# Tying the conversion of doubles and the combination of stored rows to the pieces of the last chunk

## The chip, the cores and the metric

The kernel runs on one core of one Trainium2 chip. The metric is the device time of one execution in microseconds (us); lower is better. Inputs lie in device memory in the layouts of the host function `_layout`, and the output is written back there.

## The reference

Attention of 2 x 8 heads over 576 positions that keeps the 32 largest scores of each row, then a mixture of 8 experts with gates balanced by eight Sinkhorn rounds, then a second feed-forward layer with Mish. All inputs are float32 for the first two parts. The last layer's weights are doubles in the kernel's input (`w64`, read as 64-bit words).

```python
x = attention_top32(q, k, v)                     # (1152, 512)
logits = x @ w_gate                              # (1152, 8)
P = exp(logits - logits.max())
for _ in range(8):
    P /= P.sum(1, keepdims=True) + 1e-09
    P /= P.sum(0, keepdims=True) + 1e-09
    P *= N / E
for e in range(8):
    out += P[:, e:e+1] * (maximum(x @ w1[e], 0) @ w2[e])   # 512 -> 1024 -> 512
h = out @ w_in                                   # 512 -> 2048
return (h * tanh(softplus(h))) @ w_out           # 2048 -> 512
```

## The kernel before

Tokens come in nine tiles of 128 rows. The first mixture runs over three chunks of tiles, (0, 1), (2, 3) and (4 to 8). Each chunk passes through all 8 experts, and each expert in 8 pieces of 128 hidden columns, so a chunk has 64 pieces (`ffn_pass`). A number is split into a high and a low part of a reduced float type, and a product is three matmuls (high x high, high x low, low x high).

A piece of the last chunk, whose tiles have 640 rows together, is this. Two loads bring its weights (`load_piece`, L517); ScalarE makes the high part `wh` (L520), POOL the low part `wl` of the first half and VectorE that of the second (L522). TensorE computes `h` in two groups of 320 columns, 12 matmuls each, into two PSUM buffers (`mm1`, L619). For each group ScalarE writes `hh` = relu(h) (L537) and VectorE `hl` = relu(h) - hh (L538); the PSUM buffer is free after `hl`. Two pieces later the second product (`second`, 15 matmuls at L596) adds to five PSUM banks `y`, one for each tile. After an expert's 8 pieces `combine` (L638, L640) multiplies each `y` by its gate and adds it to `acc` on VectorE.

The gates are known only when attention has ended, so the first two chunks can't do that: `spill` stores their `y` tiles in device memory, 32 rows in all (8 experts x 4 tiles). The generator `gating` (`gate_logits`, `sinkhorn`, `once_gated`) is advanced by one step at each step of the last chunk. Its end, `once_gated`, loads each stored row into `yb` (two buffers, SP's queue, L735) and combines it (L638, L640). Then it converts the doubles of the last layer's weights, 16 pieces in two halves, so 32 conversions (`double_to_float`, L689 on). A conversion loads 512 KB into `cx` (two buffers, SP's queue, L692), squares the top word on ScalarE into `cd` (L698), does six VectorE operations (L699 and L701 to L705: `cb`, `ca`, `cb`, `cc`, `cc`, `cc`) and stores `cc` on SP's queue (L706). L703 is the last reader of `cx`.

The order on TensorE is the program's. The order on every other engine and queue is a planner's: among the instructions that can go, the one with the best priority goes first, by the streams `first` (0: `hh`, `hl`), `evict` (combinations of `y`), `prep` (weights), `attn` (rows), `moe`, `fill` (conversions). `after(a, b)` adds an edge that puts a behind b in the plan, with no wait on the chip when both are on one engine. Each queue runs in its planned order: an instruction that waits holds up those behind it. Before the change the first VectorE operation of a conversion has one such edge, behind the end of the Sinkhorn rounds (`live["sunk"]`).

After the last chunk the pool of the conversions is closed and its memory goes to the last layer's pools `wq`, `hq` and `mp`. The transposes of the sums (`transposed`) for tiles 0 to 3 are issued from three quarters of the last chunk's steps on.

Of the kernel before, what the change touches and what calls it, by code (L numbers as in the profile page):

```python
# [14 lines left out]
ALU = mybir.AluOpType  # L15
# [32 lines left out]
EARLY = [(t, h) for t in (2, 3) for h in range(H)] + [(t, h) for t in (5, 6) for h in range(HG)]  # L48
EARLY_FROM, EARLY_PER_STEP = 5, 2
HOLD, RATE = 8, 0.25  # L50


class Streams:
# [19 lines left out]
def attention_moe_moe2(ctx: ExitStack, tc: tile.TileContext, qT, kT, vm, vt, wg, wst, w64, out):  # L73
    nc = tc.nc
# [5 lines left out]
    def after(inst, earlier):  # L80

        tc.add_manual_dep(
            inst.ins,
            earlier.ins.name,
            mybir.DependencyInfo(mybir.DependencyClass.NoSync, mybir.DependencyReason.DATA),
            reason="order",
        )
# [24 lines left out]
    with st("attn"):  # L112
# [8 lines left out]
        gate = const.tile([P, NT, E], F32, name="gate")  # L121
# [15 lines left out]
    def groups(n):  # L137

        k = -(-n // 512)
        return [(i * (n // k), n // k) for i in range(k)]  # L140
# [5 lines left out]
    qset, live, away = {}, {}, {}  # L146
# [227 lines left out]
    def bank1(name):  # L374
        if ps_b is None:
            return ps_a.tile([P, 512], F32, tag="tr", name=name)
        return ps_b.tile([P, 512], F32, tag="misc", name=name)

    def gate_logits(ci):

        n = P * len(CHUNKS[ci])
        lt = (const if ps_b is None else yb).tile([2 * E, n], F32, tag="lt", name=f"lt{ci}", bufs=1)
        for c0, m in groups(n):
            with st("attn"):
                ps = bank1(f"lt_{ci}_{c0}")
                k = 0
                for c in range(NC):
                    for x in x_tiles(ci):
                        nc.tensor.matmul(
                            ps[:, :m], wgs[:, c, :], x[:, c, c0 : c0 + m], start=(k == 0), stop=(k == 2 * NC - 1)  # L390
                        )
                        k += 1
                nc.scalar.activation(lt[:, c0 : c0 + m], ps[: 2 * E, :m], AF.Copy)
            yield
        with st("attn"):
            lg = bank1(f"lg_{ci}")[:, : len(CHUNKS[ci]) * 2 * E].rearrange("p (j e) -> p j e", e=2 * E)
            for j, t in enumerate(CHUNKS[ci]):
                nc.tensor.transpose(lg[:, j, :], lt[:, j * P : (j + 1) * P], ident[: 2 * E, : 2 * E])
            t0 = CHUNKS[ci][0]
            nc.scalar.activation(lg16[:, t0 : t0 + len(CHUNKS[ci]), :], lg, AF.Copy)  # L400
        yield
# [65 lines left out]
    def sinkhorn():  # L467
        with st("first"):
            nc.vector.tensor_add(gate, lg16[:, :, :E], lg16[:, :, E:])
            m1 = small.tile([P, 1], F32, tag="m1", name="m1")  # L470
            nc.vector.tensor_reduce(m1, gate.rearrange("p t e -> p (t e)"), AX.X, ALU.max)
            mb = const.tile([P, P], F32, name="mb")
            nc.vector.tensor_copy(mb, m1.to_broadcast([P, P]))
        yield
        with st("first"):
            mt = bank1("mt")[:, :P]
            nc.tensor.matmul(mt, mb, ident, start=True, stop=True)
            gm = small.tile([P, 1], F32, tag="gm", name="gm")
            nc.vector.tensor_reduce(gm, mt, AX.X, ALU.max)
            nc.vector.tensor_scalar(gm, gm, -1.0, None, op0=ALU.mult)  # L480
            nc.scalar.activation(gate, gate, AF.Exp, bias=gm)
        for i in range(8):
            with st("first"):
                rs = small.tile([P, NT], F32, tag="rs", name=f"rs_{i}")
                nc.vector.tensor_reduce(rs, gate, AX.X, ALU.add)
                nc.vector.tensor_scalar(rs, rs, EPS, None, op0=ALU.add)
                nc.vector.reciprocal(rs, rs)
                nc.vector.tensor_mul(gate, gate, rs.unsqueeze(2).to_broadcast([P, NT, E]))
            yield
            with st("first"):  # L490
                cs = bank1(f"cs_{i}")[:, : NT * E]
                nc.tensor.matmul(cs, ones, gate.rearrange("p t e -> p (t e)"), start=True, stop=True)
                cr = small.tile([P, E], F32, tag="cr", name=f"cr_{i}")
                nc.vector.tensor_reduce(cr, cs.rearrange("p (t e) -> p e t", e=E), AX.X, ALU.add)
                nc.vector.tensor_scalar(cr, cr, EPS, None, op0=ALU.add)
                nc.vector.reciprocal(cr, cr)
                nc.vector.tensor_scalar(cr, cr, float(NTOK) / E, None, op0=ALU.mult)
                live["sunk"] = nc.vector.tensor_mul(gate, gate, cr.unsqueeze(1).to_broadcast([P, NT, E]))


    acc = {}
# [24 lines left out]
    class Relu:  # L526
# [8 lines left out]
        def first(self, ps, c0, m):  # L535
            h, l = self.hh[:, c0 : c0 + m], self.hl[:, c0 : c0 + m]
            nc.scalar.activation(h, ps, AF.Relu)  # L537
            nc.vector.scalar_tensor_tensor(l, ps, 0.0, h, op0=ALU.max, op1=ALU.subtract)  # L538

        later = ()  # L540

# [93 lines left out]
    def combine(t, e, y):  # L635
        if t not in acc:
            acc[t] = accb.tile([P, DM], F32, tag=f"acc{t}", name=f"acc_{t}")
            nc.vector.tensor_scalar(acc[t], y, gate[:, t, e : e + 1], None, op0=ALU.mult)  # L638
        else:
            nc.vector.scalar_tensor_tensor(acc[t], y, gate[:, t, e : e + 1], acc[t], op0=ALU.mult, op1=ALU.add)  # L640

    def spill(t, e, y):
        ycount[0] += 1
# [9 lines left out]
    def moe_chunk(ci):  # L653
        for e in range(E):
            put = spill if ci in SPILLED else combine
            yield from ffn_pass(
                f"c{ci}e{e}",
                CHUNKS[ci],
                [wst[p] for p in range(e * EP, (e + 1) * EP)],
                *x_tiles(ci),  # L660
                Relu,
                lambda t, y, e=e, put=put: put(t, e, y),
            )
# [7 lines left out]
    begin = pos = CHUNKS[0][-1] * H + H + AHEAD + 2  # L671
# [17 lines left out]
    def double_to_float(dst, src, name):  # L689

        x = cp.tile([P, 512, 2], U32, tag="cx", name=f"cx_{name}")
        nc.sync.dma_start(x, src.bitcast(U32).rearrange("p (n w) -> p n w", w=2))  # L692
        low, top = x[:, :, 0], x[:, :, 1]
        a = cp.tile([P, 512], U32, tag="ca", name=f"ca_{name}")
        p2 = cp.tile([P, 512], U32, tag="cb", name=f"cb_{name}")
        b = cp.tile([P, 512], F32, tag="cc", name=f"cc_{name}")
        sq = cp.tile([P, 512], F32, tag="cd", name=f"cd_{name}")
        nc.scalar.activation(sq, top.bitcast(F32), AF.Square)  # L698
        begin = nc.vector.tensor_scalar(p2, top, 3, 0x3FFFFFFF, op0=ALU.logical_shift_left, op1=ALU.bitwise_and)  # L699
        after(begin, live["sunk"])  # L700
        nc.vector.scalar_tensor_tensor(a, top, 0xC0000000, p2, op0=ALU.bitwise_and, op1=ALU.bitwise_or)  # L701
        nc.vector.tensor_scalar(p2, a, 0xFF800000, None, op0=ALU.bitwise_and)
        nc.vector.scalar_tensor_tensor(b, low, 2.0**-52, p2.bitcast(F32), op0=ALU.mult, op1=ALU.mult)  # L703
        nc.vector.tensor_add(b, a.bitcast(F32), b)
        nc.vector.scalar_tensor_tensor(b, sq, TINY2, b, op0=ALU.is_ge, op1=ALU.mult)  # L705
        nc.sync.dma_start(dst, b)  # L706
# [19 lines left out]
            yield  # L726

    w32 = []

    def once_gated():  # L730

        with st("attn"):
            for t, e, d in spilled:
                y = yb.tile([P, DM], F32, tag="yback", name=f"yb_{t}_{e}")
                nc.sync.dma_start(y, d)  # L735
                combine(t, e, y)
        with st("fill"):
            for p in range(NPIECE2):
                d = dram.tile([P, PW], F32, tag=f"w32_{p}", name=f"w32_{p}")
                for a in range(PW // 512):  # L740
                    double_to_float(d[:, a * 512 : (a + 1) * 512], w64[p, :, a * 512 : (a + 1) * 512], f"{p}_{a}")
                w32.append(d)
        yield

    steps = 2 * EP * E
    first_rows = transposed(0)
    gating = chain(gate_logits(*live.pop("gate")), sinkhorn(), once_gated())
    for i, _ in enumerate(moe_chunk(len(CHUNKS) - 1)):
        next(gating, None)
        if i >= steps * 3 // 4 and i % 4 == 0:  # L750
            next(first_rows, None)
    for _ in first_rows:
# [24 lines left out]
    for ui, unit in enumerate(UNITS2):  # L777
        rows = transposed(ui + 1) if ui + 1 < len(UNITS2) else iter(())
# [67 lines left out]
```

## Time and profile before

| | |
|---|---|
| median of 3 runs | 1249.01 us (1248.32 to 1250.55) |
| profiled execution | 1249.09 us |
| its span, first to last instruction | 1247.3 us |
| mean granted TensorE clock | 0.993 |
| busy, share of the span | PE 1180.1 us (95%), DVE 858.7 (69%), ACT 648.1 (52%), POOL 546.8 (44%) |
| last chunk's first `h` | 563.3 us |
| last layer's first `h` | 1033.5 us |

PE is TensorE's matmul unit, PEld its weight loads, DVE VectorE, ACT ScalarE, SPq the queue from which the loads are issued. `L619` is line 619 of the kernel; `h_c2e` is tile `h` of chunk 2 (the last), `x24` a count. Matmuls are pipelined and their ends are modelled, so their busy times overlap; where a piece's time matters, it is taken from start to start. Records of neighbouring VectorE operations overlap by up to 0.1 us too.

### The profile page before, as it was taken

To read this page: it belongs to the slowest core of one execution; us is meant where nothing else is said; L and a number is where in the kernel's file an instruction comes from. 1 tells how busy PE (TensorE), PEld (TensorE's weight loads), DVE (VectorE), ACT (ScalarE), POOL (GpSimd) and SP (SyncE) were. 2 spreads that over 40 slices of the span, in tenths; PEclk is the share of its full clock that TensorE was granted. 3 is DMA by queue.
4 is the path that set the end of the run, shared out by engine and by line. 5 is a ranking of instruction groups with operands and counts; after the bars stand their busy time and mean duration, and the time that the engine had idled before them with its cause. 6 is when DMAs were issued, how large, how long until landed. Compare 5 with 4: busy or idle time off the path is not lost.

```text
span 1247.3 us, 20676 instructions
## 1 busy us (share of the span) xinstructions
PE 1180.1 (95%) x7267; PEld 1040.7 (83%) x7267; DVE 858.7 (69%) x1857; ACT 648.1 (52%) x1289; POOL 546.8 (44%) x424
## 2 busy tenths in 40 slices
PE   3678999999999999999999988999999999999998
PEld 2566888998889888889888777899999998889997
DVE  6999999999999999534899989952333332323221
ACT  6786777877777777653233333332323333444432
POOL 7844778877877777771112211121111212222110
PEclk9899999999999999999999999999999999999999
DMA  8444555575655555673278776632222231223201
GB/s 254 121 144 148 178 168 173 178 223 170 213 178 167 163 155 160 186 219 120 79 249 267 237 217 205 217 100 76 77 76 73 72 110 54 91 93 119 76 27 43
DMA packets 105113, 183.18 MB, mean 147 GB/s; under 512 B 14128, under 2 KB 24624, under 8 KB 105008
## 3 DMA queue, kind: packets, MB, share of 16 engines
q1 hardware_dynamic: 103712, 180.68, 46.6%
q8 instruction: 57, 0.93, 0.3%
q10 hardware_dynamic: 1296, 1.18, 0.3%
q14 instruction: 48, 0.39, 0.1%
HBM read 158.55 MB, written 23.27 MB: 146 GB/s over the span
## 4 chain that ended last, share of the span: by engine, by line
PE 66%; DVE 24%; DMA 6%; issue 2%; POOL 1%; ACT 1%; SPq 0%; POOLq 0%; ACTq 0%; DVEq 0%
PE h_c2e L619 12%; PE y_c2e L596 11%; PE h_d L619 8%; PE y_d L596 8%; PE y_c0e L596 7%; PE h_c0e L619 7%; DVE top L254 6%; DVE w L261 5%; PE h_c1e L619 4%; PE y_c1e L596 3%; DMA cx<-in_w_dram 3%; DVE em L290 2%; DVE acc L640 2%; PE pv L348 2%; PE tr L325 1%
## 5 line engine op out<-in xcount | busy, mean ns | idle before, releaser
L522 POOL TENSOR_TENSOR wl_c2e<-wraw_c2e,wh_c2e 128x512 fp32r<-128x512 f32 x64 | 90.7, 1417 | 358.8 <-ACT wh_c2e L520 332.0
L522 POOL TENSOR_TENSOR wl_c1e<-wraw_c1e,wh_c1e 128x512 fp32r<-128x512 f32 x128 | 172.5, 1372 | 52.4 <-ACT wh_c1e L520 49.3
L522 POOL TENSOR_TENSOR wl_c0e<-wraw_c0e,wh_c0e 128x512 fp32r<-128x512 f32 x128 | 171.6, 1356 | 53.0 <-ACT wh_c0e L520 49.9
L619 PE MATMUL h_c2e<-xh,wh_c2e 128*128 128x320 f32 x512 | 161.3, 315 | 14.4 <-DVE hl_c2e L538 14.2
L520 ACT ACTIVATE wh_c2e<-wraw_c2e 128x512 fp32r<-128x512 f32 x128 | 80.7, 630 | 174.5 <-PE y_c2e L596 110.3
L619 PE MATMUL h_c2e<-xl,wh_c2e 128*128 128x320 f32 x512 | 158.7, 310 | 0.0
L619 PE MATMUL h_c2e<-xh,wl_c2e 128*128 128x320 f32 x512 | 158.5, 310 | 0.0
L254 DVE MAX8 top<-w 128x8 f32<-128x576 f32 x216 | 157.7, 747 | 0.8
L596 PE MATMUL y_c2e<-wh_c2e,hh_c2e 128*128 128x512 f32 x320 | 126.6, 396 | 0.5 <-DVE acc L640 0.5
L596 PE MATMUL y_c2e<-wl_c2e,hh_c2e 128*128 128x512 f32 x320 | 125.7, 393 | 0.0
L596 PE MATMUL y_c2e<-wh_c2e,hl_c2e 128*128 128x512 f32 x320 | 125.2, 391 | 0.0
L538 DVE SCALAR_TENSOR_TENSOR hl_c2e<-h_c2e,hh_c2e 128x320 fp32r<-128x320 f32 x128 | 62.1, 485 | 87.2 <-ACT hh_c2e L537 87.0
L619 PEld LDWEIGHTS h_c2e<-xh,wh_c2e 128*128 128x128 f32 x512 | 96.6, 189 | 24.0 <-DVE hl_c2e L538 21.9
L522 POOL TENSOR_TENSOR wl_d<-wraw_d,wh_d 128x512 fp32r<-128x512 f32 x32 | 41.4, 1293 | 161.0 <-ACT wh_d L520 161.0
L520 ACT ACTIVATE wh_c0e<-wraw_c0e 128x512 fp32r<-128x512 f32 x128 | 80.4, 629 | 51.9 <-PE y_c0e L596 21.0
L261 DVE MATCH_REPLACE8 w<-top,w 128x576 f32<-128x576 f32 x144 | 106.3, 740 | 0.0
L619 PEld LDWEIGHTS h_c2e<-xl,wh_c2e 128*128 128x128 f32 x512 | 96.6, 189 | 1.8
L557 DVE TENSOR_TENSOR hl_d<-mg_d,hh_d 128x320 fp32r<-128x320 f32 (+1 forms) x48 | 31.5, 657 | 95.7 <-ACT hh_d L556 95.7
L619 PEld LDWEIGHTS h_c2e<-xh,wl_c2e 128*128 128x128 f32 x512 | 96.7, 189 | 0.0
L520 ACT ACTIVATE wh_c1e<-wraw_c1e 128x512 fp32r<-128x512 f32 x128 | 79.8, 627 | 27.7 <-PE y_c1e L596 11.3
L522 DVE TENSOR_TENSOR wl_c2e<-wraw_c2e,wh_c2e 128x512 fp32r<-128x512 f32 x64 | 47.7, 745 | 66.0 <-ACT wh_c2e L520 65.9
L520 ACT ACTIVATE wh_d<-wraw_d 128x512 fp32r<-128x512 f32 x64 | 40.4, 631 | 95.8 <-PE y_d L596 40.9
(170 smaller groups left out, 3325.5 us busy)
## 6 DMA issues: line engine op xcount, KB each, us to landing
wraw_c0e<-in_wst_dram SPq DMA_DIRECT2D x128, 256.0 KB, 3.0
wraw_c1e<-in_wst_dram SPq DMA_DIRECT2D x128, 256.0 KB, 3.0
wraw_c2e<-in_wst_dram SPq DMA_DIRECT2D x128, 256.0 KB, 2.9
cx<-in_w_dram SPq DMA_DIRECT2D x32, 512.0 KB, 4.6
wraw_d<-w SPq DMA_DIRECT2D x64, 256.0 KB, 2.7
yd<-ysp SPq DMA_DIRECT2D x32, 256.0 KB, 3.6
yb<-yd SPq DMA_DIRECT2D x32, 256.0 KB, 3.4
w<-cc SPq DMA_DIRECT2D x32, 256.0 KB, 3.2
```

Of the source, the lines that this page charges most:

```text
L254: top8 = nc.vector.max(g, src)
L261: nc.vector.match_replace(w, g, src, NEG)
L290: nc.vector.scalar_tensor_tensor(em, s, kth, e, op0=ALU.is_ge, op1=ALU.mult, accum_out=sm)
L325: nc.tensor.transpose(tr[:, c, :], em[:, j * D + c * P :][:, :P], ident)
L348: nc.tensor.matmul(pv[i * D : (i + 1) * D, pair, c0:c1], vmain[b, pair][:, i, c, :], live["at", i][:, c, c0:c1], start=(c == 0), stop=False,)
L520: nc.scalar.activation(hi, raw, AF.Copy)
L522: eng.tensor_sub(lo, raw, hi)
L538: nc.vector.scalar_tensor_tensor(l, ps, 0.0, h, op0=ALU.max, op1=ALU.subtract)
L557: nc.vector.tensor_sub(l, g, h)
L596: nc.tensor.matmul(y, h[:, j * P : (j + 1) * P], w, start=(f == 0 and k == 0), stop=(f == nf - 1 and k == 2),)
L619: nc.tensor.matmul(ps, w[:, c * P : (c + 1) * P], x[:, c, c0 : c0 + m], start=(k == 0), stop=(k == 3 * NC - 1),)
L640: nc.vector.scalar_tensor_tensor(acc[t], y, gate[:, t, e : e + 1], acc[t], op0=ALU.mult, op1=ALU.add)
```

## The change

An instruction for each stored row (its `combine`) and for each conversion (its first VectorE operation) is kept in two lists. While the last chunk is issued, the program counts its pieces. At piece n, `pace(n)` puts the next ones of the lists behind the piece's second `hl`: one row at each piece from 11 on, and two conversions at every three pieces from 11 on. Nothing else of the kernel is changed.

```diff
+FILL_FROM = 11
...
-            nc.vector.scalar_tensor_tensor(l, ps, 0.0, h, op0=ALU.max, op1=ALU.subtract)
+            live["hl"] = nc.vector.scalar_tensor_tensor(l, ps, 0.0, h, op0=ALU.max, op1=ALU.subtract)
...
     def combine(t, e, y):
...
-            nc.vector.tensor_scalar(acc[t], y, gate[:, t, e : e + 1], None, op0=ALU.mult)
+            return nc.vector.tensor_scalar(acc[t], y, gate[:, t, e : e + 1], None, op0=ALU.mult)
...
         begin = nc.vector.tensor_scalar(p2, top, 3, 0x3FFFFFFF, op0=ALU.logical_shift_left, op1=ALU.bitwise_and)
         after(begin, live["sunk"])
+        paced["doubles"].append(begin)
...
+    paced = {"rows": [], "doubles": []}
+    held = dict.fromkeys(paced, 0)
+
+    def pace(n):
+
+        for kind, ahead in (("rows", n - FILL_FROM + 1), ("doubles", (n - FILL_FROM) * 2 // 3 + 1)):
+            for inst in paced[kind][held[kind] : max(ahead, 0)]:
+                after(inst, live["hl"])
+                held[kind] += 1
...
                 nc.sync.dma_start(y, d)
-                combine(t, e, y)
+                paced["rows"].append(combine(t, e, y))
...
+    last, pieces = live["hl"], 0
     for i, _ in enumerate(moe_chunk(len(CHUNKS) - 1)):
         next(gating, None)
+        if live["hl"] is not last:
+            last = live["hl"]
+            pace(pieces := pieces + 1)
```

## Rows read from the trace of the kernel before

**Rows 1.** By stretch: start:end, length, each engine's busy us (x instructions), clock, DMA

```profile
619.28:822.78 203.50, 188.63 (x1015) 165.17 (x1014) 189.44 (x319) 68.33 (x134) 41.51 (x26) 0.99 0.70 224
822.78:1012.64 189.86, 189.86 (x1070) 172.75 (x1069) 61.32 (x105) 58.77 (x116) 34.89 (x27) 1.00 0.26 78
```

**Rows 2.** The same view, instructions of L619 alone

```profile
619.28:822.78 203.50, 101.16 (x624) 94.29 (x624) 0.99 0.70 224
```

**Rows 3.** One undisturbed piece by stretch; chain of work there (start, length)

```profile
836.71:843.68 6.97, 6.97 (x40) 6.33 (x39) 1.68 (x3) 2.03 (x4) 1.29 (x1) 1.00 0.26 80
...
836.88 3.52 PE h_c2e L619 x24
```

**Rows 4.** Waits of PEld, 619.28 to 822.78: total us, times, longest

```profile
PEld h_c2e L619 <- DVE hl_c2e L538: 21.9, 22, 2.4
```

**Rows 5.** Groups of VectorE by shape, 619.28 to 822.78: busy, mean | idle before

```profile
L704 DVE TENSOR_TENSOR cc<-ca,cc 128x512 f32<-128x512 f32 x32 | 26.9, 841 | 0.0
L705 DVE SCALAR_TENSOR_TENSOR cc<-cd,cc 128x512 f32<-128x512 f32 x32 | 25.6, 799 | 0.0
...
L640 DVE SCALAR_TENSOR_TENSOR acc<-yb,gate,acc 128x512 f32<-128x512 f32 x28 | 24.9, 888 | 2.3 <-DMA yb<-yd 2.3
L703 DVE SCALAR_TENSOR_TENSOR cc<-cx,cb 128x512 f32<-128x512 uint32 x32 | 23.9, 747 | 0.3 <-DMA w<-cc 0.3
L701 DVE SCALAR_TENSOR_TENSOR ca<-cx,cb 128x512 uint32<-128x512 uint32 x32 | 22.8, 715 | 0.0
...
L702 DVE TENSOR_SCALAR cb<-ca 128x512 uint32<-128x512 uint32 x32 | 16.4, 514 | 0.0
L699 DVE TENSOR_SCALAR cb<-cx 128x512 uint32<-128x512 uint32 x30 | 12.6, 420 | 9.3 <-DMA cx<-in_w_dram 9.1
```

**Rows 6.** Waits of ScalarE, 619.28 to 822.78: total us, times, longest

```profile
ACT cd L698 <- DMA cx<-in_w_dram: 55.6, 18, 5.6
ACT wh_c2e L520 <- PE y_c2e L596: 26.3, 12, 3.0
```

**Rows 7.** Timeline, 783 to 793, VectorE, ScalarE, POOL: start, length, instruction

```profile
783.83 0.67 DVE L703 SCALAR_TENSOR_TENSOR cc<-cx,cb 128x512 f32<-128x512 uint32 x1
...
790.93 1.75 DVE L703 SCALAR_TENSOR_TENSOR cc<-cx,cb 128x512 f32<-128x512 uint32 x1
...
792.61 0.48 DVE L538 SCALAR_TENSOR_TENSOR hl_c2e<-h_c2e,hh_c2e 128x320 fp32r<-128x320 f32 x1
...
789.13 0.68 ACT L698 ACTIVATE cd<-cx 128x512 f32<-128x512 f32 x1 [2.75 <-DMA cx<-in_w_dram]
789.72 0.43 ACT L537 ACTIVATE hh_c2e<-h_c2e 128x320 fp32r<-128x320 f32 x1
...
790.73 1.41 POOL L522 TENSOR_TENSOR wl_c2e<-wraw_c2e,wh_c2e 128x512 fp32r<-128x512 f32 x1 [8.11 <-ACT wh_c2e L520]
```

**Rows 8.** Timeline of the undisturbed piece at 836.71: VectorE and POOL

```profile
841.33 0.49 DVE L538 SCALAR_TENSOR_TENSOR hl_c2e<-h_c2e,hh_c2e 128x320 fp32r<-128x320 f32 x1 [1.70 <-ACT hh_c2e L537]
...
841.04 1.29 POOL L522 TENSOR_TENSOR wl_c2e<-wraw_c2e,wh_c2e 128x512 fp32r<-128x512 f32 x1 [5.68 <-ACT wh_c2e L520]
```

**Rows 9.** Loads of cx, 619 to 823: KB each, median us to landing

```profile
cx<-in_w_dram SPq DMA_DIRECT2D x30, 512.0 KB, 4.6
```

**Rows 10.** Timeline: first and last of 21 pairs of L703 and Square

```profile
623.03 0.68 DVE L703 SCALAR_TENSOR_TENSOR cc<-cx,cb 128x512 f32<-128x512 uint32 x1
...
629.62 0.68 ACT L698 ACTIVATE cd<-cx 128x512 f32<-128x512 f32 x1 [2.54 <-DMA cx<-in_w_dram]
...
804.43 0.68 DVE L703 SCALAR_TENSOR_TENSOR cc<-cx,cb 128x512 f32<-128x512 uint32 x1
...
806.40 0.43 ACT L537 ACTIVATE hh_c2e<-h_c2e 128x320 fp32r<-128x320 f32 x1
...
809.70 0.69 ACT L698 ACTIVATE cd<-cx 128x512 f32<-128x512 f32 x1 [2.87 <-DMA cx<-in_w_dram]
```

**Rows 11.** Timeline of ScalarE: the first split weight of the second MoE

```profile
1003.18 0.62 ACT L520 ACTIVATE wh_d<-wraw_d 128x512 fp32r<-128x512 f32 x1
```

More of the change, by code (lines that the diff above doesn't have):

```diff
@@ L637, in combine @@
             acc[t] = accb.tile([P, DM], F32, tag=f"acc{t}", name=f"acc_{t}")
-            nc.vector.tensor_scalar(acc[t], y, gate[:, t, e : e + 1], None, op0=ALU.mult)
+            return nc.vector.tensor_scalar(acc[t], y, gate[:, t, e : e + 1], None, op0=ALU.mult)
         else:
-            nc.vector.scalar_tensor_tensor(acc[t], y, gate[:, t, e : e + 1], acc[t], op0=ALU.mult, op1=ALU.add)
+            return nc.vector.scalar_tensor_tensor(acc[t], y, gate[:, t, e : e + 1], acc[t], op0=ALU.mult, op1=ALU.add)
     def spill(t, e, y):
```

## The prediction

> **What bounds the kernel now.** I read the profile in this order: busy time by stretch, the waits of the engine that the stretch needs most, the groups of instructions of the engine that it waits for, and then single instructions.
>
> The busy time by stretch comes first [rows 1]. The last chunk begins at 563 us, and its 64 pieces each issue 24 matmuls at L619. From 619.28 to 822.78 TensorE is busy 188.63 of 203.50 us. In the next stretch, 822.78 to 1012.64, it is busy for all of its 189.86 us. VectorE is the other way round: 189.44 us busy in the first stretch, 61.32 in the second. The first stretch holds 624 matmuls of L619, which are 26 pieces [rows 2]. A piece that nothing disturbs takes 6.97 us, 3.52 of them for L619 [rows 3]. So 26 pieces could take 26 x 6.97 = 181.2 us; they take 203.5. **The stretch loses 22.3 us**, 0.86 a piece, and this is all that the change can reach. The waits agree: the weight loads of L619 wait 21.9 us, 22 times, for `hl` of L538 on VectorE [rows 4], because a PSUM bank of `h` is free only when `hl` has read it.
>
> Why is `hl` late? VectorE's own sum answers it. Its 189.4 us of work exceed the 181.2 us that 26 undisturbed pieces would last; with 9.3 us more in front of L699, where it waits for a load, its queue is full [rows 1, 5]. So here VectorE sets the pace, and the cause is that the 32 conversions and the 32 stored rows stand in 26 pieces. ScalarE adds to it: its queue stood 55.6 us behind loads of `cx` [rows 6]. One such place shows how. L703 ends at 784.5 and frees a buffer, but the Square that waits for the load into it runs on ScalarE at 789.13, and `hh` of the next group, which stood behind it, only at 789.72; `hl` follows at 792.61 [rows 7].
>
> **The change, part by part.** No instruction is added or removed on any engine; only places in queues move. `pace(n)` is called with n from 1 to 64. It ties row n - 10 behind the second `hl` of piece n, for n = 11 to 42, and 32 conversions behind those of pieces 11 to 58, two for every three pieces.
>
> Work moved on VectorE. An undisturbed piece costs it 61.32 / 27 = 2.27 us [rows 1]. The 26 crowded pieces would have cost 59.0 of that, so conversions and rows together cost 189.4 - 59.0 = 130.4 us. By the groups, the six operations of a conversion sum to 129 us for 32 (26.9 + 25.6 + 23.9 + 22.8 + 16.4, and 12.6 x 32/30) and the rows to 28 [rows 5]. The durations overlap a little, so I share out 130.4 in that ratio: 3.35 us a conversion and 0.73 a row. After the change a piece from 11 to 42 costs 2.27 + 0.73 + 2/3 x 3.35 = 5.2 us of 6.97, and one from 43 to 58 costs 4.5. Even a piece with a whole conversion and a row costs 6.35. Before, it was 189.4 / 26 = 7.29. So VectorE stops being the bound, and the 22.3 us become reachable.
>
> What covers the ties. In an undisturbed piece that begins at 836.71 the second `hl` ends at 841.82, or T + 5.1, if T is the piece's start [rows 8]. Its bank is wanted by the second group of the next piece, at T + 6.97 + 3.52 / 2 = T + 8.73, so `hl` may come 3.6 us late for nothing. Behind the tied instruction on VectorE stand the next piece's `wl` and `hl`. A row of 0.7 and a conversion of 3.35 behind `hl` end near T + 9.2, but they are six or seven short operations, and `hl` has the better priority: it stands behind one of them, at most 1.8 us with the longest row [rows 7]. If that cover were gone, each of some 48 pieces could lose up to 1 us.
>
> The queues that the moved steps also use. A conversion issues a load of `cx` (512 KB) and a store on SP's queue and a Square on ScalarE; a row issues a load of `yb` on SP. The loads wait for a buffer that the tied instruction frees, so they move along with the ties. L703 of a tied conversion ends about 3.2 us after `hl` (row, L699, L701, L702, L703, and 0.6 for a `wl` among them), at T + 8.3. The load lands 4.6 us later [rows 9], at T + 12.9. The next use of that buffer on VectorE is tied some three pieces later, so VectorE's 9.3 us in front of L699 go. On SP, weight loads stand behind these; the same loads stood there before, and the waits of ScalarE in this stretch name no load of weights [rows 6], so a load that blocks SP for some us is covered. On ScalarE the Square can hold up `hh`. Where it stands in the queue decides this. Of the L703 that stand between the second `hl` of one piece and the first `hl` of the next, 21 have a Square two conversions later; the first is at 623.03 with its Square at 629.62, the last at 804.43 with its Square at 809.70, behind the `hh` at 806.40 [rows 10]. In 19 of the 21 that Square stands behind both `hh` of the next piece. Tied L703 all lie in this gap. Then the Square has until T + 2 x 6.97 + 1.76 = T + 15.7, when the `hh` behind it is due, and the data are there at T + 12.9. I cost it at nothing, from below at zero, from above with the rival below.
>
> The ends. The last row is tied to piece 42, and the transposes that read the sums are issued from three quarters of the steps on, at piece 49. The last conversion begins at T + 5.1 of the 58th piece and ends about 5 us later. The buffers of the conversions go over to the second MoE, whose first weights are split on ScalarE at 1003.18, in the 60th piece at T + 4.5 [rows 11]: some 8 us later. If it came late, `hh` behind it would have 3.6 us of cover. Nothing here.
>
> What I leave as loss: six expert ends lie in pieces 11 to 58, where five combinations of 0.74 us come on top. I take 0.5 us for each, 3 us in all; the bounds are 0 (the undisturbed stretch has the same expert ends, and loses nothing) and the 16 us of the second case.
>
> **The sum.** The profiled execution took 1249.1 us (span 1247.3), the median of the runs is 1249.0. 1249.1 - 22.3 + 3 = 1229.8, against the median **1229.7 us**. Not below 1226.5: the rest of the program is not touched.
>
> **The rivals.** *Half of it stays.* L703 at 790.93 took 1.75 us where 0.68 is usual; POOL's `wl` ran from 790.73 to 792.14 [rows 7]. So each operation of VectorE that meets POOL's loses about 1.1 us, and with the work spread, every piece may have one. The piece with a conversion and a row then costs 6.35 + 1.1 = 7.5, 0.5 over. With the five combinations of some pieces and order errors I make it 0.75 over in each of the 21 pieces of 11 to 42 that have a conversion: 16 us, 1243 us. Against it: the third piece of each three has room, `hl` has 3.6 us of cover, and POOL's operation runs at T + 4.3 to 5.6, mostly beside `hl` [rows 8], which reads PSUM. The Trainium skill (SBUF — State Buffer, Who interferes with whom) has a rule for this: a VectorE operation with two SBUF inputs and a GpSimd operation exclude each other for a whole instruction. The trace agrees, with the 1.75 us above. Chance 0.14, 1235 to 1246.
>
> *Slower: the tie closes a loop.* If the Square stands before the second `hh` of the next piece (2 of the 21), a late load makes that `hh` late, this the `hl`, and this the next tied conversion. Load at T + 12.9, Square 0.6, `hh` 0.45, `hl` 0.5: `hl` at T + 14.5, where T + 12.1 is usual, 2.4 us late. Two conversions in neighbouring pieces make 4.8, over the cover of 3.6 by 1.2; 16 such pairs lose 19 us, and the gain is gone: 1246. The point from which it is slower is a load of 4.7 us instead of 4.6. At 5.5 us, which the traffic of weights could bring, it is 2 x 3.3 - 3.6 = 3.0, 48 us in all: **1275 us**. Against it: 19 of 21, and that the memory traffic gets thinner as it is spread. Chance 0.07 for slower, and 0.05 for a result within 0.2% of before, which also holds the next one.
>
> *The ties bind nothing.* The order would be as before: 1249. Against it: the thirtieth conversion has its L703 at 804.43 [rows 10], in the 32nd piece, and its tie is the 55th. It is nearly excluded.
>
> **How the numbers follow.** Forecast 0.74 (1226.5 to 1235), half 0.14, no change 0.05, slower 0.07. A measurement of this kernel can tell 0.2%, 2.5 us, from no change. Faster 0.74 + 0.14 = 0.88, same 0.05, slower 0.07. From 1226.5 to 1242 lie the first case and over half of the second, about 0.82.
>
> **What would show it.** Right: pieces 9 to 58 at 6.97 us each (but for the four with transposes), `hl` waits of the weight loads under 4 us, VectorE near 75% from 640 to 850 and 65% after it, the last L705 in the 58th or 59th piece, TensorE's end of the chunk some 19 us earlier. Wrong: new waits of L619 for `hl` between 822 and 990 us, Squares right ahead of an `hh` that wait for `cx`, or a first wait in the second MoE.

## The result and the profile after

The changed kernel takes 1228.27 us (median of 4 runs, 1226.21 to 1230.47) against 1249.78 us of the kernel before in the same comparison. The ratio is 0.983, with a 95% interval of 0.981 to 0.985: some 21 us faster. The forecast was 1229.7. The profiled execution took 1226.21 us, with a span of 1224.4.

Busy time by stretch after the change: first the 26 pieces that answer to the crowded stretch of [rows 1] (pieces 9 to 34), then 640 to 850 and 850 to 1000 us. Columns are as there.

```profile
618.91:800.21 181.30, 181.30 (x1015) 164.76 (x1014) 125.81 (x210) 62.23 (x119) 34.24 (x26) 1.00 0.55 173
...
640.00:850.00 210.00, 210.00 (x1177) 190.91 (x1177) 153.70 (x257) 74.02 (x141) 39.42 (x30) 1.00 0.60 189
850.00:1000.00 150.00, 150.00 (x850) 136.66 (x849) 92.30 (x158) 53.41 (x103) 27.68 (x21) 1.00 0.44 139
```

TensorE is busy for all of the 181.30 us; the same 26 pieces took 203.50. From start to start every piece from the 9th to the last takes 6.97 us, but for four of 7.41 with the transposes. VectorE has 125.81 us of work there, 4.8 a piece; from 640 to 850 us it is busy 73%, from 850 to 1000 us 62%.

The waits of the weight loads in the whole last chunk, which answer to [rows 4], are now only those of the gates:

```profile
PEld cs L493 <- PE y_c2e L597: 1.6, 3, 0.6
PEld cs L493 <- PE h_c2e L620: 1.0, 4, 0.3
PEld lg L399 <- issue: 0.2, 1, 0.2
```

No `hl` is waited for any more; it was 21.9 us. The groups of VectorE from 640 to 850 us (busy, mean | idle before) show where the meetings with POOL went, and where its room is:

```profile
L641 DVE SCALAR_TENSOR_TENSOR acc<-yb,gate,acc 128x512 f32<-128x512 f32 x27 | 29.8, 1103 | 0.0
L539 DVE SCALAR_TENSOR_TENSOR hl_c2e<-h_c2e,hh_c2e 128x320 fp32r<-128x320 f32 x60 | 29.3, 488 | 37.1 <-ACT hh_c2e L538 37.1
...
L706 DVE TENSOR_TENSOR cc<-ca,cc 128x512 f32<-128x512 f32 x20 | 13.7, 686 | 0.1
```

A row's addition has a mean of 1103 ns (888 in [rows 5]; 740 is usual), while L706, which was L704 with 841 ns, takes its usual 686. And `hl` now waits for ScalarE for 37.1 us: VectorE is early. ScalarE itself still waits for loads (total, times, longest), less than in [rows 6], though the view covers all conversions:

```profile
ACT cd L699 <- DMA cx<-in_w_dram: 38.8, 29, 3.6
```

Single instructions of the piece that begins at 660.75 us (VectorE, POOL, ScalarE) show the tie at work, and what a row pays:

```profile
665.36 0.49 DVE L539 SCALAR_TENSOR_TENSOR hl_c2e<-h_c2e,hh_c2e 128x320 fp32r<-128x320 f32 x1 [0.95 <-ACT hh_c2e L538]
665.76 1.16 DVE L641 SCALAR_TENSOR_TENSOR acc<-yb,gate,acc 128x512 f32<-128x512 f32 x1
...
665.08 1.30 POOL L523 TENSOR_TENSOR wl_c2e<-wraw_c2e,wh_c2e 128x512 fp32r<-128x512 f32 x1 [5.68 <-ACT wh_c2e L521]
...
666.19 0.67 ACT L699 ACTIVATE cd<-cx 128x512 f32<-128x512 f32 x1 [0.87 <-DMA cx<-in_w_dram]
...
669.74 0.44 ACT L538 ACTIVATE hh_c2e<-h_c2e 128x320 fp32r<-128x320 f32 x1 [1.19 <-PE h_c2e L620]
```

The row starts right behind the second `hl`, while POOL makes `wl` (665.08 to 666.38), and takes 1.16 us. The Square at 666.19 stands behind both `hh` of its piece and far ahead of the next one, at 669.74; nobody waits for it. The end of the conversions and the first weight of the second MoE on ScalarE (VectorE, ScalarE) are 4.5 us apart:

```profile
975.50 0.69 DVE L707 SCALAR_TENSOR_TENSOR cc<-cd,cc 128x512 f32<-128x512 f32 x1
...
980.73 0.62 ACT L521 ACTIVATE wh_d<-wraw_d 128x512 fp32r<-128x512 f32 x1
```

### The profile page after: what moved, and what is told of

It is laid out like the page before. It is cut to its first block, busy times and chain, and to the rows that moved or that the text cites. A ratio compares the mean times of both kernels' runs of the same rounds, so it can differ in the third digit from the quotient of the medians.

```text
span 1224.4 us, 20740 instructions
## 1 busy us (share of the span) xinstructions
PE 1172.0 (96%) x7267; PEld 1040.0 (85%) x7267; DVE 858.1 (70%) x1857; ACT 652.7 (53%) x1289; POOL 540.1 (44%) x424
## 4 chain that ended last, share of the span: by engine, by line
PE 80%; DVE 15%; DMA 2%; ACT 1%; POOL 1%; issue 1%; SPq 0%; POOLq 0%; ACTq 0%
PE h_c2e L620 18%; PE y_c2e L597 18%; PE h_d L620 8%; PE y_d L597 8%; PE y_c0e L597 7%; PE h_c0e L620 7%; DVE top L255 6%; DVE w L262 5%; PE h_c1e L620 4%; PE y_c1e L597 4%; DVE em L291 2%; PE pv L349 2%; PE tr L326 1%; DMA kraw<-in_kT_dram 1%; PE sc L227 1%; PE pv L356 1%
## 5 line engine op out<-in xcount | busy, mean ns | idle before, releaser
L523 POOL TENSOR_TENSOR wl_c2e<-wraw_c2e,wh_c2e 128x512 fp32r<-128x512 f32 x64 | 84.0, 1312 | 344.3 <-ACT wh_c2e L521 344.3
L620 PE MATMUL h_c2e<-xh,wh_c2e 128*128 128x320 f32 x512 | 158.2, 309 | 0.0
L538 ACT ACTIVATE hh_c2e<-h_c2e 128x320 fp32r<-128x320 f32 x128 | 54.9, 429 | 76.5 <-PE h_c2e L620 75.4
```

The lines of the kernel that those rows point to most:

```text
L523: eng.tensor_sub(lo, raw, hi)
L620: nc.tensor.matmul(ps, w[:, c * P : (c + 1) * P], x[:, c, c0 : c0 + m], start=(k == 0), stop=(k == 3 * NC - 1),)
```

## The experiments

Line numbers in kernels made from the changed one are one or two higher than before the change. "Lost" below is the length of pieces 9 to 34 less the 181.3 us that they take in the changed kernel; for later pieces it is reckoned in the same way.

**One half of the change at a time.** In `e1_rows_only` the conversions' tie is left out:

```diff
-        paced["doubles"].append(begin)
```

> Theory A (VectorE's queue): the 22 us were lost because 26 pieces held 189 us of VectorE work, where 181 fit. Theory B (ScalarE's waits): they were lost because Squares that wait for loads of cx stand ahead of hh on ScalarE. Here only the rows are tied; the conversions stay packed. A: the 26 crowded pieces lose some 16 of the 32 rows or less, VectorE's work there falls from 189 to about 183 us, its waits stay: about 1242 us (1236 to 1246). B: the loads and Squares are as before: 1247 to 1250.

Measured: 1247.18 us, ratio 0.999 (0.997 to 1.000). Pieces 9 to 34, and VectorE's wait for loads of `cx` there:

```profile
618.99:822.50 203.51, 190.58 (x1016) 169.28 (x1014) 178.00 (x310) 68.83 (x134) 42.93 (x26) 0.97 0.68 215
...
DVE cb L700 <- DMA cx<-in_w_dram: 18.6, 17, 2.8
```

The expectation of 1242 failed, and 1247 is what theory B had said. VectorE's work falls from 189.4 to 178.0 us, less than the 181.2 that the pieces need, and yet they take 203.5 as before. The conversions moved closer together into the room of the rows (the last one starts in piece 31 instead of 33), and waited 18.6 us for their loads, 9.1 before. Work and these waits together, 196.6 us, are still above the limit. So a sum of work below the limit does not help by itself.

In `e2_conversions_only` only the conversions are tied:

```diff
-                paced["rows"].append(combine(t, e, y))
+                combine(t, e, y)
```

> Only the conversions are tied; the 32 rows stay packed right after the Sinkhorn rounds, some 2.5 rows a piece. A: a piece there costs VectorE 2.3 + 1.8 + 2.2 = 6.3 us of 6.97, so little is lost: 1228 to 1231. B: the Squares wait for nothing that matters: 1228. If the rows had been the cause of the loss, 1240 or more.

Measured: 1238.09 us, ratio 0.992 (0.989 to 0.995). The same 26 pieces, and VectorE's waits for loads of `yb`:

```profile
621.48:815.34 193.86, 185.81 (x1015) 165.23 (x1014) 130.82 (x218) 61.14 (x119) 35.69 (x26) 0.99 0.55 172
...
DVE acc L641 <- DMA yb<-yd: 15.3, 14, 2.9
...
DVE acc L639 <- DMA yb<-yd: 4.2, 1, 4.2
```

It missed by 7 us at least. All 12.6 us are lost in pieces 10 to 18, where the rows stand. VectorE is busy only 130.8 us of 193.9, but rows at the head of its queue wait 19.5 us for loads into two buffers. No run gives `yb` more buffers, so that these loads are the whole of this loss is read from the waits and not shown. Both halves of the change are needed: 1247 with rows alone, 1238 with conversions alone, 1228 with both.

**ScalarE's waits.** `e3_no_square` is the kernel before without the Square:

```diff
-        nc.scalar.activation(sq, top.bitcast(F32), AF.Square)
...
-        nc.vector.scalar_tensor_tensor(b, sq, TINY2, b, op0=ALU.is_ge, op1=ALU.mult)
+        nc.vector.scalar_tensor_tensor(b, a.bitcast(F32), NEG, b, op0=ALU.is_ge, op1=ALU.mult)
```

> The kernel before without the Square on ScalarE. Left out: values below the smallest normal number are no longer set to zero; the last of the six VectorE operations compares another tile instead, so VectorE does the same work. A: VectorE's 189 us and its own waits for cx stay, so 8 to 20 us stay lost: 1236 to 1248. B: hh never stands behind a load, and nearly all of the 22 us come back: 1228 to 1232.

Measured: 1247.91 us, ratio 0.998 (0.997 to 1.000).

```profile
618.98:819.09 200.11, 187.72 (x1015) 163.37 (x1014) 186.69 (x319) 52.75 (x104) 45.24 (x26) 1.00 0.71 228
...
DVE cb L697 <- DMA cx<-in_w_dram: 8.5, 10, 2.1
...
ACT hh_c2e L537 <- PE h_c2e L619: 43.9, 26, 3.0
```

ScalarE waits for TensorE's `h` (43.9 us) and for no `cx` at all, 55.6 us before, and 18.8 of the 22.2 us stay lost. Squares ahead of `hh` were not the main cause; theory B falls.

**Loads.** `e4_four_load_buffers` is the kernel before with four buffers:

```diff
-        x = cp.tile([P, 512, 2], U32, tag="cx", name=f"cx_{name}")
+        x = cp.tile([P, 512, 2], U32, tag="cx", name=f"cx_{name}", bufs=4)
```

> The kernel before with four buffers for cx instead of two, nothing tied: loads are made two conversions earlier. A: the waits for cx go from VectorE (9 us) and ScalarE (56 us), the work of 189 us in as few pieces stays or gets denser: 1236 to 1249. B: with the waits the loss goes: 1228 to 1231.

Measured: 1237.96 us, ratio 0.991 (0.987 to 0.994).

```profile
621.03:816.70 195.67, 186.63 (x1015) 165.44 (x1014) 186.03 (x319) 70.81 (x134) 45.15 (x26) 0.99 0.70 228
...
PEld h_c2e L619 <- DVE hl_c2e L538: 11.7, 13, 2.9
```

VectorE waits for no `cx`, and some 11 us come back by the medians. The profiled execution was the longest of its four (1242.58 us); in it 14.4 us are still lost. `e8_rows_and_buffers` puts this edit and that of `e1_rows_only` together:

> Rows tied, conversions free, but four buffers for cx. With rows alone tied the conversions moved closer together and waited 18.6 us for loads on VectorE (9.1 before), which gave the rows' gain back. A: with the loads ahead too, VectorE has about 180 us of work and no waits in the 26 pieces: 1229 to 1235, below the 1238 of the four buffers alone. If the rows don't matter at all: 1238. If the conversions just move closer together again: 1238 or more.

Measured: 1239.02 us, ratio 0.993 (0.991 to 0.995).

```profile
620.03:812.05 192.02, 184.69 (x1015) 164.10 (x1014) 179.50 (x310) 71.00 (x134) 45.03 (x26) 1.00 0.69 223
...
PEld h_c2e L620 <- DVE hl_c2e L539: 9.7, 11, 2.2
```

By the medians this is no better than the buffers alone. VectorE's work is 179.5 us, below the limit, and it waits for no `cx`; 10.7 us are lost. With this run theory A fails as a sum of work over the stretch, and the rest needs another cause.

**Meetings with POOL.** What was left were VectorE operations of over 1 us: 23 in the 26 pieces of the kernel before, 19.8 us over 0.7 each; 25 in `e8_rows_and_buffers`, 15.3 us over. Each overlaps POOL's `wl`, as in [rows 7].

The sum over 26 pieces also hides that they differ. Pieces 11, 19 and 27, where an expert's five combinations come on top, lose 5.6 of the 10.7 us of `e8_rows_and_buffers`. Over its pieces 9 to 31 VectorE's busy time exceeds 6.97 us a piece by 7.2 us, and with 3.6 us of waits for DMA that is the loss. In the kernel before it is 10.5 us over pieces 10 to 31, with 11.7 us of waits. So VectorE's queue does set the pace. But with the operations of over 1 us counted at 0.7, no row of consecutive pieces exceeds its time by more than 1.6 us (1.8 in the kernel before), and `hl` may come 3.6 us late. What is too much is the length that meetings and waits add, and not the work or its uneven spread.

In the last two experiments on the kernel before, VectorE makes that `wl` too, so nothing of POOL's runs in these pieces. `e9_no_collisions` does it with four buffers, `e12_no_meetings_two_buffers` with two:

```diff
-            eng = nc.vector if (a and ps_b is not None) else nc.gpsimd
+            eng = nc.vector if ((a or tag.startswith("c2")) and ps_b is not None) else nc.gpsimd
```

> The kernel before with four buffers for cx, and in the last chunk VectorE also makes the low part wl that POOL made: 0.7 us more VectorE work a piece, but nothing of POOL's runs beside it. Theory A (the sum of VectorE's work stretches the crowded pieces): 18 us more work in 26 pieces, so as slow as four buffers alone or slower, 1238 to 1250. Theory C (untied conversions fill VectorE's order up to what the planner believes fits; what stretches a piece is only what the planner did not count, the 1.1 us of a meeting with POOL and late loads): the planner counts the added work and spreads the conversions over more pieces, the meetings are gone, so most of the remaining loss goes: 1228 to 1234.

Measured: 1230.28 us, ratio 0.985 (0.983 to 0.987).

```profile
623.59:806.29 182.70, 182.35 (x1015) 164.50 (x1014) 177.80 (x335) 70.94 (x134) 0.00 (x0) 1.00 0.75 241
...
L704 DVE TENSOR_TENSOR cc<-ca,cc 128x512 f32<-128x512 f32 x30 | 20.5, 683 | 0.0
...
PEld h_c2e L619 <- DVE hl_c2e L538: 1.5, 4, 0.8
```

VectorE is fuller than in any other run, 177.8 of 182.7 us (97%), has one more operation in each piece, and loses 1.4 us. L704 takes 683 ns in the mean, where it took 841 [rows 5].

> The kernel before with wl of the last chunk wholly on VectorE, two buffers for cx as before: the fourth corner beside before (1249.5), four buffers (1238) and both (1230). Theory C, with the two causes adding up: the meetings are worth the 8 us between 1238 and 1230, the late loads stay: 1240 to 1243. If the meetings alone were the cause: 1230. If the late loads alone: 1249 or more.

Measured: 1232.05 us, ratio 0.986 (0.983 to 0.989).

```profile
618.27:804.53 186.26, 183.44 (x1015) 164.37 (x1014) 172.47 (x323) 69.08 (x132) 0.00 (x0) 1.00 0.73 234
...
DVE cb L699 <- DMA cx<-in_w_dram: 10.2, 11, 2.0
...
PEld h_c2e L619 <- DVE hl_c2e L538: 5.4, 8, 1.1
```

The expectation of 1240 to 1243 failed on the good side. The loads' waits are as long as before (10.2 us), and yet only 5.0 us are lost in these pieces. So the two causes don't add up. I read this so: with nothing else late, `hl`'s cover swallows most of a late load. Both kernels change two things, the meetings and VectorE's order, which is planned anew: 28 conversions begin in these pieces here and 30 with four buffers, as before the change; 28 and 30 end there, and 32 before. The loss fell although VectorE has more work than the 169.6 us (189.4 - 19.8) that the kernel before has without its meetings. That the meetings and not the new order did this is therefore likely, but no run changes one of them alone.

One table for all of these, pieces 9 to 34 of the profiled execution. The second column sums VectorE's operations of over 1 us, less 0.7 us each, from the single instructions; the third sums its waits for any DMA. Each row is one execution; it was the longest of four for `conversions only`, `four buffers` and the two without meetings, and the shortest for `no Square`, `rows and buffers` and `changed`.

| kernel | VectorE busy | meetings | waits for DMA | lost |
|---|---|---|---|---|
| rows only | 178.0 | 13.2 | 18.6 | 22.2 |
| before | 189.4 | 19.8 | 11.7 | 22.2 |
| no Square | 186.7 | 17.0 | 11.1 | 18.8 |
| four in three (below) | 170.3 | 13.9 | 12.7 | 18.3 |
| conversions only | 130.8 | 6.4 | 19.5 | 12.6 |
| four buffers | 186.0 | 16.5 | 4.8 | 14.4 |
| rows and buffers | 179.5 | 15.3 | 3.6 | 10.7 |
| no meetings, two buffers | 172.5 | 0 | 12.2 | 5.0 |
| no meetings, four buffers | 177.8 | 0 | 3.3 | 1.4 |
| one a piece (below) | 152.7 | 9.9 | 0 | 0 |
| changed | 125.8 | 8.2 | 0 | 0 |

The loss goes with the sum of the two middle columns, some 0.4 to 0.7 of it, and not with the busy time. In the last two rows, where the ties leave room, meetings cost nothing.

**How dense may the ties be?** `e5_one_a_piece` and `e6_four_in_three` change the rate alone:

```diff
-        for kind, ahead in (("rows", n - FILL_FROM + 1), ("doubles", (n - FILL_FROM) * 2 // 3 + 1)):
+        for kind, ahead in (("rows", n - FILL_FROM + 1), ("doubles", (n - FILL_FROM) + 1)):
...
+        for kind, ahead in (("rows", n - FILL_FROM + 1), ("doubles", (n - FILL_FROM) * 4 // 3 + 1)):
```

> The changed kernel with one conversion tied at every piece (pieces 11 to 42) instead of two at every three. Theory A in the form that the first four runs leave (a piece is stretched when VectorE's queue, its work and the loads it waits for, takes longer than 6.97 us): a piece costs VectorE 2.3 + 0.7 + 3.35 = 6.35 us, and the load for a conversion two pieces on is there in time: 1228 to 1231. If the width of the spread itself mattered, a third of the way back to before: 1235.

Measured: 1228.05 us, ratio 0.984 (0.981 to 0.987), as the changed kernel.

```profile
621.67:802.80 181.13, 181.13 (x1015) 164.64 (x1014) 152.71 (x258) 66.36 (x127) 34.87 (x26) 1.00 0.65 209
...
DVE hl_c2e L539 <- ACT hh_c2e L538: 17.0, 19, 1.7
```

> The changed kernel with four conversions tied at every three pieces (pieces 11 to 34), rows one a piece as before. A: 2.3 + 0.7 + 4.5 = 7.5 us of VectorE for 6.97, so each of some 24 pieces is stretched by 0.5 us or more, and two conversions behind one hl wait for each other's loads: 1240 (1235 to 1249). If the place behind hl were what matters and not the density: 1228.

Measured: 1247.38 us, ratio 1.000 (0.998 to 1.001): all of the gain is gone.

```profile
619.72:819.32 199.60, 187.89 (x1016) 165.01 (x1014) 170.31 (x292) 66.99 (x131) 41.15 (x25) 0.99 0.66 209
...
DVE cb L700 <- DMA cx<-in_w_dram: 9.3, 10, 1.8
```

The limit is sharp. At one conversion a piece VectorE is busy 152.7 of 181.1 us (84%), still stands 17.0 us for `hh`, and nothing is lost; at four in three the order fills up again (from piece 15 to 34 VectorE is busy 142.8 of 157.8 us), loads are waited for, and 18.3 us are lost here and 2.1 later. The place behind `hl` alone buys nothing.

**The slower rival.** `e7_square_first` puts on ScalarE the second `hh` of the next piece behind the Square of the conversion two further on:

```diff
...
     def pace(n):
+        while due:
+            after(live["hh"], squares[due.pop()])
...
                 held[kind] += 1
+                if kind == "doubles" and held[kind] + 1 < len(squares):
+                    due.append(held[kind] + 1)
```

> The changed kernel with one more tie: the second hh of the next piece stands on ScalarE behind the Square that waits for the next load of cx (the loop of the slower rival). By the rival with the load that the changed kernel shows, 4.0 us instead of 4.6: hl comes 1.8 us late for a conversion, 3.6 for two in a row, just the cover of 3.6: 1228 to 1232. With the 4.6 us of the prediction: 1246. If ScalarE's queue is closer to the limit than thought, more.

Measured: 1251.16 us, ratio 1.002 (1.000 to 1.004). One turn of the loop (SP's queue, ScalarE, VectorE; then TensorE's waits from 740 to 772 us):

```profile
758.17 0.33 SPq L693 DMA_DIRECT2D cx<-in_w_dram  x1
...
762.81 0.66 ACT L699 ACTIVATE cd<-cx 128x512 f32<-128x512 f32 x1 [3.65 <-DMA cx<-in_w_dram]
763.38 0.75 ACT L538 ACTIVATE hh_c2e<-h_c2e 128x320 fp32r<-128x320 f32 x2
...
763.83 0.49 DVE L539 SCALAR_TENSOR_TENSOR hl_c2e<-h_c2e,hh_c2e 128x320 fp32r<-128x320 f32 x1 [3.64 <-ACT hh_c2e L538]
...
PE h_c2e L620 <- DVE hl_c2e L539: 4.1, 1, 4.1
```

The load is issued at 758.17, the Square stands before it for 3.65 us and holds up both `hh`; `hl` follows at 763.83 and TensorE has stood for 4.1 us. 14.0 us are lost in pieces 9 to 34 and 12.4 later: the whole gain and more. `e11_square_first_buffers` keeps this order and takes four buffers for `cx`:

> The kernel with the Square tied ahead of the second hh, which was slower than before (1251), with four buffers for cx: the load that the Square waits for is issued two conversions earlier. If the loop through the load made that kernel slow: 1228 to 1231. If Squares ahead of hh cost time in themselves: 1240 or more.

Measured: 1230.75 us, ratio 0.986 (0.983 to 0.988).

```profile
PEld h_c2e L620 <- DVE hl_c2e L539: 1.8, 4, 0.6
```

1.8 us of waits are left. So the loop through the late load was the cost, and not the place of the Square.

**A candidate.** `e10_after_no_meetings` is the changed kernel with `wl` of the last chunk on VectorE, the edit of `e12_no_meetings_two_buffers`:

> The changed kernel with wl of the last chunk wholly on VectorE, as a candidate that could beat both. If meetings with POOL were the cause of the loss, the changed kernel has none left to win in the tied pieces (5.2 + 0.7 us of VectorE in 6.97 leave room): 1228. The first pieces with the Sinkhorn rounds took 54.4 instead of 56.0 us where POOL was left out, so 1226 to 1227 at best, within 0.2% of the changed kernel. If VectorE gets too full: 1230 or more.

Measured: 1225.13 us, ratio 0.982 (0.979 to 0.985).

```profile
616.49:797.62 181.13, 181.13 (x1015) 164.65 (x1014) 132.62 (x236) 61.59 (x119) 0.00 (x0) 1.00 0.56 175
```

The tied pieces lose nothing, as in the changed kernel; the first eight pieces take 54.5 instead of 56.0 us. The intervals of the two kernels overlap, so that it beats the changed one is not shown.

## Why the prediction was right, and where its reason was not

- *What can be won.* The stretch lost 22.3 us and the change could reach only that [rows 1 to 3]. Right: these pieces take 181.3 us now, 0.1 over the 181.2. The last layer's first `h` comes 22.5 us earlier (1011.1 against 1033.5).
- *The residue.* I left 3 us for six expert ends. This term was mis-sized: it measured 0, as its lower bound said.
- *VectorE's cost after the change.* 5.2 us a piece from 11 to 42 (75%) and 4.5 later (65%) were forecast; 73% and 62% were measured.
- *Why `hl` was late.* This step failed in its reason. That VectorE's queue was full and set the pace was right: its busy time beyond TensorE's (10.5 us) and its waits for DMA (11.7 us) make up the loss. But I took busy time for work, and so the packing of conversions and rows for the cause. Of the 189.4 us, 19.8 came from meetings with POOL; without them 169.6 us are left, which fit into 181.2. In `no meetings, four buffers` as many conversions begin in the 26 pieces as before, VectorE is busy 177.8 us, and only 1.4 were lost; in `rows and buffers` it is busy 179.5 us, and 10.7 were lost. What did not fit were lengths that came on top of the work: meetings and waits for DMA. The forecast's number did not hang on this step, since the 22.3 us were read from TensorE's time, and the ties leave room for both. That the planner fills the order by lengths that leave these out is argued from the runs; its own lengths were not looked at.
- *The half-way rival.* It named the right mechanism and put it at the wrong place. Rows do meet POOL's `wl` (1103 ns instead of 740), but in a piece with room this costs nothing. It was the kernel before that the meetings made slow. The rule of the Trainium skill that stood there (SBUF — State Buffer, Who interferes with whom) is given on its page for a GpSimd instruction that reads SBUF, as `wl` does. It agrees with the runs: where POOL made no `wl` in the last chunk, no VectorE operation of pieces 9 to 34 took over 1 us.
- *Loads and Squares.* The load landed in 4.0 us (median of the 30 issued from 619 us on) instead of 4.6. The last reads of `cx` (L705 now, L703 before) were all to lie between a second `hl` and the next first one; 29 of the 32 do. Of the 28 of these with a Square two conversions on, 21 have that Square behind both `hh` of the next piece, and 7 behind the first alone; 19 of 21 had been read from the order before. The Square at 756.68 us is one of the 7: the second `hh` starts behind it at 757.77, 4.35 us after the first where 2.1 is usual. This stayed within the cover, and no Square held up TensorE.
- *The slower rival.* The mechanism exists, and the reading that rejected it was right in the main: only 7 of 28 places of the changed kernel have that order, and TensorE lost nothing there. Its price was too small. For a load of 4.6 us I had 19 us and a point of no gain at 4.7; with loads of 4.3 us (median) the loop lost 26.4 us. A single turn stood 4.1 us.
- *The ends.* No wait appears at the transposes or in the second MoE. The last conversion ends 4.5 us ahead of the first split weight of the second MoE; some 8 us had been worked out. Four combinations of an expert's end stand among its operations, and it takes 8.4 us instead of 5.

## What to carry to other kernels

Filling work of low priority should be tied to the loop that it hides in, at a rate that leaves the filled engine some room. Here 84% full lost nothing, and a third more conversions lost all of the gain; how much room is needed depends on what comes on top, since without the meetings a VectorE that was 97% full lost only 1.4 us. A busy sum over the limit is not yet a cause: look for single operations that take twice their usual time and for loads at the head of a queue, since these are what a fixed order does not foresee. Give each half of such a change a run of its own; the room that one half frees may be filled by the other.

## What the runs showed of the hardware

A VectorE operation of a row or a conversion that meets POOL's `wl` takes up to 1.8 us instead of 0.7 (1.82 in the kernel before). `hl`, which reads one input from PSUM, does not: 60 of them overlap an operation of POOL in the last chunk of the changed kernel, and none takes over 0.5 us. Moving that `wl` to VectorE, with more work on the fuller engine, took 17 us off the kernel before (1249 to 1232). I had not expected the meetings to weigh so much.

The start of the last chunk moved between 562.0 and 569.2 us over the profiled executions, with no edit ahead of it in several of them. This spread is of the size of the differences between the best kernels here, so these were read from the pieces and not from the total.
